# Attention and low-rank mixer on one core: all batches in a replanned order, loads of two queues charged in issue order, early copies on GpSimd

## The chip, the cores and the metric

The kernel runs on 1 core of one Trainium2 chip. The metric is the device time of one execution in microseconds. Several executions are timed and the median is given. A profile of one execution is at hand as well; its times count from the start of the profiled span.

The engines have short names: PE is TensorE (matrix products), ACT is ScalarE, DVE is VectorE, POOL is GpSimd, SP is SyncE. POOL and SP also issue DMA transfers, each on a queue of its own: the casting loads go through POOL's queue, plain copies and stores through SP's.

## What is computed

For 4 batches, 8 heads, 768 positions and head width 64: attention with a local window of 96 keys and 8 global keys, with a bias linear in the distance; then, on the 512-wide rows of all heads, a mixer along the sequence of rank 32 and a two-layer MLP of width 2048, both with a residual.

```python
scores = scale * np.matmul(q, k.transpose(0, 1, 3, 2))
scores = np.where(keep, scores + bias, -1e9)
a = softmax(scores)
x = (a @ v) rearranged to [batch, seq, heads * width]
h = x^T @ U @ V
u = x + h^T
out = u + relu(u @ w_ch1) @ w_ch2
```

Inputs and output are fp32.

## The kernel before

**Tasks.** The kernel is a list of 1107 named tasks. A task is a handful of instructions on one engine, with what it depends on and the buffers that it takes and gives back. `ORDER` is a list of all names, written out. `Planner.run` walks it once, gives every task a start from durations held in the code, chooses buffer slots and PSUM banks on the way, and returns the tasks sorted by those starts; in that order the instructions are issued, so each engine works its own tasks in the order in which `ORDER` has them. Real waits are semaphores that follow from the data. Where the plan shows a gap on PE in the opening, `idle` fills it with matmuls on zeros (line 1327).

**Names.** The work goes over 16 head pairs p (4 a batch), then an MLP a batch b.

- Loads: `lk`, `lq`, `lv` with p, `w1_i`, `w2_i` (quarters of the weights), `mixl` (U and V of the mixer, on SP, behind `back`, which follows `EK1`). Pair 0's k and q come over SP as fp32 and are cast by `Ck0`, `Cq0`; all other loads are casting DMAs issued by POOL. From pair 4 on `lk` and `lq` are two transfers each. Staging buffers hold 3 pairs of k and q and 4 of v.
- Attention: `TK`, `TQ` transpose on PE, `EK`, `EQ` evacuate them, `KO` builds keys with the global ones in front, `VC`, `VG` the same for v. `SB` puts the bias into PSUM (batch 0), `S` adds the scores, `EX` is the exponential on ACT, `MK` the mask (later batches), `PV` the product with v, `RC` reciprocal and `NM` normalization on DVE, `XC` the cast of the result to fp16 (for pair 3 `NH` in three parts).
- Mixer: `UP` starts u in PSUM and forms x U; `TE` evacuates the small product, `HM` multiplies it by V (`vs0`, `vs1`, `vs2` are fp16 halves of V and their difference), `E0`, `E1` evacuate u. `HR` says for each pair whether `HM` uses all 128 rows (F) or 64 (R, two products side by side in the array). 
- MLP: the first layer as plain products `M1` with `RL`, `RM` (ReLU), and from batch 1 partly as seven-product blocks `ZP` with sums on DVE and ACT (`Z...`, `PA`, `PB`, `TW`, `TD`). The second layer is `RS`, then `P1` to `P7` for each of three column tiles t, added to x by `DA` to `DH` on DVE, and stored by `O` on SP. In the last batch, tile 2, `P4` and `DG` are cut in two (`a`, `b`) with stores of their own.

**Which engine.** Strings in `CFG` give, for each pair, the engine of a copy: A is ACT, D is DVE, P is POOL, S a DMA on SP, Q a DMA on POOL. `VO` sets `VC` and `VG`, `XC` the cast of x, `VS` the three vs tasks.

**The plan's DMA model.** A task with a `size` is a transfer. Each of the two queues has a time from which it is free; a transfer on SP also pushes POOL's queue back. The tasks are charged in the order of `ORDER`, not of their starts.

**Array forms.** `S` and `RS` and `HM` in form R use 64 rows, `TK`, `TQ` of pairs 1 to 3 use 64 columns, all else the whole array.

Of the kernel before, what the change touches and what calls it, by code (L numbers as in the profile page):

```python
# [36 lines left out]
XU5 DA0.1 P30.1 DF0.1 mask4 MK6.1 MK6.2 P50.0 lv6 lq9 VC7 TE5 HM5 mask6 KO8 S6.0 EX6.0 E05 P60.0 DB0.0 lk9 mask7
lk10 lv8 P60.1 DB0.1 lv11 S7.1 RS0.2 EX7.1 MK6.0 MK7.0 EX7.2 MK7.2 P10.2 P70.0 TK9 EK9 TQ9 EQ9 MK7.1 VC6 DA0.2 VG6
TQ10 EQ10 P50.1 TK10 EK10 P70.1 DC0.0 lq11 VG7 PV7 DD0.1 KO9 PV6 RC7 NM7 P20.2 XC7 lk11 RC6 NM6 P60.2 DB0.2 P30.2
UP7 XC6 VC8 VG8 P40.1 UP6 P70.2 XE6 XU6 TE6 ZS4 XE7 XU7 lk12 TE7 DD0.0 P40.0 DC0.1 O0.1 HM6 E06 HM7 E17 DF0.2 DG0.1  # L40
ZP11.5 DD0.2 P40.2 ZU1.5 DG0.0 E07 ZT1 S8.0 EX8.0 S8.1 O0.0 EX8.2 EX8.1 KO10 P50.2 M1a1.3 TK11 DC0.2 EK11 O0.3
# [5 lines left out]
RM1.5 ZP51.6 HM8 E08 ZA1.7 ZX1.6 TK12 TD1 EK12 ZP41.7 ZR1.7 M1a1.5 RL1.5 VG9 ZB1.6 ZP51.7 ZB1.7 M1a1.0 ZV1.6 M1b1.0
RL1.0 ZV1.7 ZP31.6 M1a1.1 M1b1.1 MK9.0 lq12 TQ12 ZP31.7 VC11 ZP41.6 VG11 ZD1.6 ZQ1.6 EQ12 ZD1.7 ZQ1.7 RL1.1 ZR1.6
PA1.3 RS1.1 S10.1 EX10.2 EX10.1 PA1.0 PB1.0 S10.0 EX10.0 PB1.3 KO12 P21.1 P11.1 PV9 P51.1 RC9 NM9 PB1.1 DA1.1 S11.0
EX11.0 RS1.0 P21.0 P51.0 P11.0 DA1.0 XC9 S11.1 EX11.2 EX11.1 MK11.0 P31.0 DF1.0 MK11.2 P61.1 MK10.0 UP9 XE9 lq14  # L50
TQ14 EQ14 MK11.1 P31.1 DF1.1 P61.0 DB1.0 XU9 TE9 PV11 RC11 lk14 TK14 EK14 lk15 HM9 DB1.1 P71.0 E09 P71.1 lv14 VC14
# [1327 lines left out]
```

## Time and profile before

| | us |
|---|---|
| median of 3 runs (225.2 to 225.95) | 225.79 |
| the profiled execution | 225.68 |
| its span | 223.9 |
| first filler matmul starts | 0.94 |
| first product (`SB0`) starts | 3.09 |
| last task of batch 0's attention before the MLP (`S4.1`) ends | 30.9 |
| last matmul starts | 220.33 |
| last store lands | 223.0 |

The granted clock of PE is 1.00 over the whole span. The page gives the busy time of each engine, the chain of work that ended last and groups of instructions by line; the timeline gives single instructions in order. Matmuls overlap: one that is shown with 0.326 us starts 0.163 us behind the one before it, so the distance between starts tells more than the busy time. In the waits view a line reads: engine and line, what it waited for, total us, how many times, the longest. In the view by stretches a line has the stretch, its length, then busy time (and instructions) of PE, weight loads, DVE, ACT and POOL, the PE clock, the DMA share and GB/s.

### The profile page before, as it was taken

To read this page: it belongs to the slowest core of one execution; us is meant where nothing else is said; L and a number is where in the kernel's file an instruction comes from. 1 tells how busy PE (TensorE), PEld (TensorE's weight loads), DVE (VectorE), ACT (ScalarE), POOL (GpSimd) and SP (SyncE) were. 2 spreads that over 40 slices of the span, in tenths; PEclk is the share of its full clock that TensorE was granted. 3 is DMA by queue.
4 is the path that set the end of the run, shared out by engine and by line. 5 is a ranking of instruction groups with operands and counts; after the bars stand their busy time and mean duration, and the time that the engine had idled before them with its cause. 6 is when DMAs were issued, how large, how long until landed. Compare 5 with 4: busy or idle time off the path is not lost.

```text
span 223.9 us, 6008 instructions
## 1 busy us (share of the span) xinstructions
PE 217.5 (97%) x2446; PEld 160.8 (72%) x2446; DVE 182.3 (81%) x407; ACT 143.5 (64%) x251; POOL 68.9 (31%) x90
## 2 busy tenths in 40 slices
PE   8997999999999999999999999999999999999993
PEld 3754876675888976666788886666688976658883
DVE  5876957889998887997987888788888995888892
ACT  6889697887877378787855567668732347882000
POOL 8876976634964400191221400012000000000000
PEclk9999999999999999999999999999999999999999
DMA  6999999999999987399090941609100104000035
GB/s 172 174 176 146 181 182 185 193 206 161 169 149 73 157 151 223 97 115 71 0 107 12 108 123 52 200 12 70 39 3 3 47 3 187 0 4 0 0 116 215
DMA packets 88763, 23.97 MB, mean 107 GB/s; under 512 B 76416, under 2 KB 86528, under 8 KB 88736
## 3 DMA queue, kind: packets, MB, share of 16 engines
q0 software_dynamic: 69888, 13.64, 73.8%
q1 hardware_dynamic: 18848, 9.95, 15.7%
q8 instruction: 19, 0.31, 0.6%
q14 instruction: 8, 0.07, 0.1%
HBM read 27.46 MB, written 6.29 MB: 151 GB/s over the span
## 4 chain that ended last, share of the span: by engine, by line
PE 90%; DMA 4%; POOL 2%; issue 1%; ACT 1%; DVE 0%; DVEq 0%; POOLq 0%
PE ps L1226 34%; PE ps L1095 14%; PE ps L1000 13%; PE ps L1024 8%; PE ps L716 4%; DMA stgq<-in_q_dram 4%; PE ps L594 4%; PE ps L822 3%; PE ps L849 2%; PE ps L848 2%; PE ps L946 2%; PE ps L1327 1%; PE ps L1218 1%; PE ps L697 1%; POOL stgk L454 1%
## 5 line engine op out<-in xcount | busy, mean ns | idle before, releaser
L781 ACT ACTIVATE ep<-ps 128x1024 f16<-128x1024 f32 (+1 forms) x48 | 43.9, 952 | 14.8 <-PE ps L716 14.5
L1226 PEld LDWEIGHTS <-htr 128*128 128x128 f16 x392 | 36.2, 98 | 6.7 <-issue 2.3
L1238 DVE TENSOR_TENSOR x_sb<-x_sb,ps 128x256 f32<-128x256 f32 (+1 forms) x60 | 26.9, 464 | 7.5 <-PE ps L1226 7.1
L1000 PE MATMUL ps<-uT,w 128*128 128x384 f16 x176 | 32.4, 326 | 0.0
L1226 PEld LDWEIGHTS <-sA 128*128 128x128 f16 x288 | 27.3, 98 | 3.5
L458 POOL DMA_DIRECT2D vt<-in_v_dram x16 | 16.6, 1046 | 30.7 <-PE ps L849 27.3
L1000 PEld LDWEIGHTS <-w 128*128 128x128 f16 x176 | 16.7, 98 | 10.5
L1226 PE MATMUL ps<-w,sA 128*128 128x256 f16 x192 | 24.2, 273 | 0.0
L1226 PE MATMUL ps<-tB,htr 128*128 128x256 f16 (+1 forms) x200 | 23.8, 268 | 0.0
L1226 PE MATMUL ps<-w,htr 128*128 128x256 f16 x192 | 23.5, 273 | 0.0
L1006 ACT ACTIVATE htr<-ps 128x384 f16<-128x384 f32 x44 | 20.8, 492 | 4.1 <-PE ps L1000 3.5
L454 POOL DMA_DIRECT2D stgk<-in_k_dram x24 | 19.8, 845 | 9.9 <-PE ps L594 5.0
L454 POOL DMA_DIRECT2D stgq<-in_q_dram x24 | 20.0, 844 | 5.6 <-DMA w<-in_moe_w_ch_dram 3.4
L1024 PE MATMUL ps<-uT,w 128*128 128x384 f16 x112 | 21.3, 326 | 0.0
L1113 DVE TENSOR_TENSOR htr<-ps,zu 128x384 f16<-128x384 f32 x30 | 16.1, 554 | 6.1 <-PE ps L1095 4.6
L794 DVE TENSOR_TENSOR ep<-ep,mask 128x1024 f16<-128x1024 f16 x24 | 15.9, 684 | 2.9 <-ACT ep L781 2.9
L359 ACT ACTIVATE zu<-ps 128x384 f32<-128x384 f32 x30 | 14.4, 492 | 4.2 <-PE ps L1095 4.0
L887 DVE TENSOR_TENSOR x_sb<-ps,rcp 128x768 f32<-128x768 f32 x16 | 15.2, 953 | 0.4
L1024 PEld LDWEIGHTS <-w 128*128 128x128 f16 x112 | 10.6, 98 | 6.8
L1095 PEld LDWEIGHTS <-w 128*128 128x128 f16 x108 | 10.1, 98 | 6.2 <-issue 0.3
L1042 ACT ACTIVATE htr<-ps 128x768 f16<-128x768 f32 x14 | 11.3, 811 | 4.7 <-PE ps L1024 4.5
L716 PE MATMUL ps<-qT,kT 64*128 64x128 f16 x192 | 14.0, 217 | 0.0
(127 smaller groups left out, 442.3 us busy)
## 6 DMA issues: line engine op xcount, KB each, us to landing
out_dram<-x_sb SPq DMA_DIRECT2D x17, 256.0 KB, 2.4
w<-in_moe_w_ch_dram POOLq DMA_DIRECT2D x8, 512.0 KB, 10.6
vt<-in_v_dram POOLq DMA_DIRECT2D x16, 192.0 KB, 6.6
stgk<-in_k_dram POOLq DMA_DIRECT2D x24, 96.0 KB, 5.8
stgq<-in_q_dram POOLq DMA_DIRECT2D x24, 96.0 KB, 6.1
out_dram<-x_sb SPq DMA_DIRECT2D x13, 128.0 KB, 1.9
...
```

The source lines that it names most:

```text
L454: nc.gpsimd.dma_start(o[:, i], src[b, h0 + i].rearrange("(n p) d -> p n d", p=P))
L458: nc.gpsimd.dma_start(vt[gv.slot][:, :, :, 0:D], v[b, h0:h0 + 2].rearrange("h (n p) d -> p h n d", p=P),)
L716: nc.tensor.matmul(t[:, hi, j * P:(j + 1) * P], lhs, qt[r, i * P:(i + 1) * P], start=not biased, stop=True, skip_group_check=biased,)
L781: nc.scalar.activation(ep[gep.slot][:, :, lo:512], ps[:, gsc.slot:gsc.slot + 2, lo:512], AF.Exp, scale=qk_scale)
L794: nc.vector.tensor_tensor(ev, ev, mv, ALU.mult)
L1000: nc.tensor.matmul(ps[:, g.slot, 0:HS], w1[:, dc, jt * P:(jt + 1) * P], ub[:, dc, i * HS:(i + 1) * HS], start=(dc == 0), stop=(dc == NDC - 1),
L1006: nc.scalar.activation(htr[:, jt, i * HS:(i + 1) * HS], ps[:, g.slot, 0:HS], AF.Relu)
L1024: nc.tensor.matmul(ps[:, g.slot + half, 0:HS], w1[:, dc, jt * P:(jt + 1) * P], ub[:, dc, half * HS:(half + 1) * HS], start=(dc == flat[0]) ...
L1095: nc.tensor.matmul(bank(g), a()[:, i], bq[:, i], start=first and i == 0, stop=last and i == 1, skip_group_check=True,)
L1113: return lambda: nc.vector.tensor_tensor(o, x(), y(), ALU.add)
L1226: nc.tensor.matmul(o if part is None else o[:, part], a[:, j, c0 + cols.start:c0 + cols.stop], bq[:, j] if part is None else bq[:, j, part ...
L1238: nc.vector.tensor_tensor(o, o, x, ALU.add)
```

## The change

`ORDER` is a new permutation of the same 1107 names, for all batches. In the plan, a transfer may not start before the last one issued on the other queue has started (`issued`), so that a transfer must stand in `ORDER` where it is issued; POOL's queue is taken to be free from 5.6 instead of 6.1. `mixl` stands ahead of `lk4` now, and was behind `w1_2`.

`CFG` moves copies: `VC`, `VG` of pairs 1 and 2, `vs0`, `vs1` and `XC` of pair 2 go to POOL, which made none before; `VC6`, `VG6` go to ACT. Other copies change between ACT, DVE and SP. `HR` turns pairs 0, 2 and 9 from F to R. `RC` of a pair waits for `NM` two pairs earlier (the two share a buffer); both are DVE's. `VS` can name a DMA on POOL, which this setting does not use.

Array forms change 72 times in the new order of PE's tasks and 77 times in the old one.

```diff
--- before.py
+++ after.py
 ORDER = """
-lk0 ones2 wz iota lq0 lk1 ones0 vz relf lq1 rel3 lk3 lq2 bias1 ones3 lv0 bias0 SB0.2 SB0.1 Ck0.1 Cq0.0 bias2 bias4
-Ck0.0 TK0 EK0.1 lk2 Cq0.1 TQ0 EQ0.0 SB0.0 lq3 EK0.0 KO0.1 KO0.0 EQ0.1 mask1 S0.0 EX0.0 TK1 S0.1 EX0.1 EK1 S0.2 KO1
-TQ1 EQ1 ones1 lv1 back SB1.1 TK3 EK3 KO3 VC0 mask5 VG0 EX0.2 lk5 lv3 lv2 lq5 lk4 SB1.2 S1.1 EX1.1 S1.2 TQ2 EQ2 lq4
-SB1.0 w1_0 S1.0 EX1.0 TK2 EK2 KO2 lk7 VC1 w1_3 PV0 RC0 EX1.2 lv4 VG1 TQ3 EQ3 SB2.1 S2.1 EX2.1 lq6 SB2.2 S2.2 EX2.2
-PV1 NM0 SB3.0 S3.0 EX3.0 RC1 NM1 SB2.0 S2.0 w1_2 EX2.0 mixl u16 XC0 VC2 VC3 VG3 SB3.1 S3.1 EX3.1 SB3.2 S3.2 EX3.2
-VG2 vs0 vs1 TK5 EK5 XC1 TQ5 PV2 RC2 NM2 UP0 TE0 TK4 EK4 UP1 TE1 XC2 EQ5 HM0 E00 PV3.0 PV3.1 PV3.2 RC3.2 RC3.0 NH3.2
-TQ4 EQ4 NH3.0 UP2 TE2 HM1 E01 HM2 E02 RC3.1 NH3.1 KO4 NM3 UP3.0 UP3.1 UP3.2 TE3 M1a0.3 M1c0.3 mask0 HM3 E03 KO5 S4.1
-E13 EX4.1 lq7 M1d0.3 TK7 M1b0.3 RL0.3 M1b0.14 M1b0.15 M1a0.2 M1c0.2 M1a0.15 EX4.2 M1a0.13 vs2 TD0 M1a0.14 MK4.2 VC4
-VG4 w1_1 RM0.15 RM0.14 RL0.15 mask2 S4.0 EX4.0 MK4.1 EK7 M1d0.2 M1b0.2 RL0.2 MK4.0 RL0.14 M1b0.13 mask3 KO7 ZS5
-M1a0.10 M1b0.12 RM0.12 RM0.13 RL0.10 TQ6 PV4 M1a0.11 M1b0.11 RL0.13 EQ6 RC4 NM4 XC4 TQ7 EQ7 ZS7 RL0.11 RM0.11 lk6
-lv5 S5.0 S5.1 EX5.0 MK5.0 EX5.2 M1a0.8 M1b0.10 RM0.10 PA0.3 PB0.3 M1a0.9 RL0.9 w2_2 EX5.1 MK5.1 M1b0.5 RM0.5 M1a0.0
...
-M1a3.4 RL3.4 M1b3.5 RM3.5 ZP33.6 RS3.0 ZV3.6 ZD3.6 ZQ3.6 PA3.3 RS3.1 PA3.0 RS3.2 P23.2 P23.0 ZQ3.3 ZQ3.2 P13.1 P13.2
-PA3.1 P13.0 DA3.1 DA3.0 P53.2 P63.0 P53.1 PB3.0 P63.1 P53.0 DA3.2 P63.2 P23.1 PB3.2 PB3.3 DB3.0 PB3.1 DF3.2 P73.0
-DB3.1 P73.1 DB3.2 P33.2 DD3.0 O3.2a O2.0 DC3.0 DC3.2 P33.1 DC3.1 DH3.2 O3.2 DD3.1 P33.0 DF3.1 O3.1 DF3.0 O3.0 P73.2
-DD3.2 O3.5a P43.0 DG3.0 O3.3 P43.1 DG3.1 O3.4 P43.2a P43.2b DG3.2a O3.5b DG3.2b O3.5c
+ones1 wz lk0 iota relf rel3 ones3 lk1 bias1 bias0 SB0.0 lq1 lk3 ones0 lv0 bias2 Ck0.0 bias4 Ck0.1 vz TK0 EK0.0 lk2
+lq2 KO0.0 lv1 lq0 Cq0.1 Cq0.0 SB0.1 SB0.2 TQ0 EQ0.0 lq3 ones2 lv2 EK0.1 KO0.1 EQ0.1 lv3 TK1 EK1 KO1 back S0.1 TQ1
+EQ1 S0.0 mask1 mixl EX0.1 S0.2 TK3 EK3 VC0 KO3 VG0 lk4 EX0.2 lk5 EX0.0 VC1 VG1 lq4 VC2 VG2 vs1 SB1.0 SB1.1 S1.1
+SB1.2 S1.2 EX1.1 S1.0 EX1.0 TK2 EK2 KO2 TQ2 lq5 vs0 w1_3 EQ2 PV0 RC0 SB2.2 EX1.2 NM0 SB2.1 S2.1 EX2.1 XC0 S2.2 EX2.2
+TQ3 EQ3 PV1 RC1 SB2.0 S2.0 EX2.0 NM1 u16 SB3.1 S3.1 EX3.1 XC1 SB3.2 S3.2 EX3.2 SB3.0 S3.0 EX3.0 VC3 VG3 PV2 RC2 UP0
+TE0 mask0 NM2 XC2 TK4 EK4 w1_0 PV3.0 PV3.1 PV3.2 RC3.0 NH3.0 RC3.1 NH3.1 HM0 E00 lv4 RC3.2 NH3.2 UP1 TE1 UP2 TE2 TQ4
+EQ4 TK5 NM3 EK5 HM2 E02 HM1 UP3.0 KO4 UP3.1 UP3.2 TE3 TQ5 E01 EQ5 S4.0 HM3 E03 E13 KO5 EX4.0 w1_2 S4.1 EX4.2 lq7
+M1a0.13 RL0.13 M1a0.14 lk7 M1b0.15 M1a0.15 RL0.14 lq6 vs2 M1b0.14 M1b0.13 M1a0.3 M1c0.3 M1d0.3 w1_1 VC4 VG4 MK4.2
+lv5 mask2 EX4.1 MK4.1 RM0.14 RM0.13 M1b0.12 RL0.15 M1a0.2 M1c0.2 M1b0.3 M1d0.2 M1b0.2 RM0.15 MK4.0 RM0.12 ZS7 PV4
+RC4 TQ7 EQ7 NM4 M1b0.11 mask3 RL0.3 RL0.2 lk6 M1a0.11 TK7 EK7 KO7 M1a0.10 RM0.11 RL0.11 XC4 TQ6 EQ6 ZS5 S5.0 RL0.10
+EX5.0 S5.1 EX5.2 MK5.2 EX5.1 M1b0.8 RM0.8 M1a0.0 w2_2 w2_0 M1c0.0 M1d0.0 M1b0.10 M1a0.6 RM0.10 M1b0.0 M1a0.5 RL0.6
...
+ZV3.3 M1a3.5 ZP73.6 ZP53.6 PB3.2 ZP33.7 ZD3.7 ZX3.6 ZQ3.7 RL3.5 M1a3.1 M1b3.1 ZB3.6 RL3.1 ZP43.6 ZP33.3 ZR3.6 ZV3.6
+M1a3.4 ZP23.6 ZP33.6 ZD3.3 RS3.0 RL3.4 ZV3.7 ZD3.6 ZA3.6 ZQ3.6 PA3.3 RS3.1 O2.0 ZQ3.3 RS3.2 P23.2 ZQ3.2 PA3.1 P23.1
+P23.0 PA3.0 P13.0 DA3.0 P13.2 PB3.1 P13.1 DA3.1 P53.2 P53.0 DA3.2 P63.2 PB3.0 PB3.3 DC3.2 P63.1 DC3.0 P53.1 DC3.1
+DB3.2 P33.1 P33.0 DF3.0 P63.0 DB3.0 O3.0 P33.2 P73.0 DF3.1 DB3.1 O3.1 DD3.0 P73.2 DD3.2 O3.5a DH3.2 P43.0 DG3.0 O3.3
+P73.1 O3.2 DD3.1 P43.2a DF3.2 O3.2a P43.2b P43.1 DG3.2a O3.5b DG3.2b O3.5c DG3.1 O3.4
 """.split()
 CFG = {
...
-    "ZR": "DDAADDDA", "ZQ": "DDAADDDD", "TE": "ADAAAAAAAAAAAADA", "XE": "DDDDDAADADAADAAA", "EK": "ADDDDDADADADDAAD", "EQ": "DDAAAADDAAADDAAD", "KO": "ADDDDDADSSSSASDS",
-    "HR": "FRFRRRRRFFRRFRRR", "IB": "AAAA", "U16": "A", "VS": "DAD", "C0": "ADDADADA", "DL": (), "SPL": (0,), "BI": (0, 1, 2, 3), "EKS": "ADDADADA", "EQS": "DDDADADA", "KOS": "ADDADADA",
-    "VO": "DDDDDDDSSSSSDSSS", "XC": "DDDDDAAADADQADQA", "E": "AAAAAAAAAAAAAAAA",
+    "ZR": "DDDADADA", "ZQ": "DDAADDDD", "TE": "AAADAAADAAAAAAAA", "XE": "DDDDDAAAAAAAAADA", "EK": "ADDDADADAAADDDAD", "EQ": "DDADADDDAAADAAAA", "KO": "ADDDDDSDSASSSSAD",
+    "HR": "RRRRRRRRFRRRFRRR", "IB": "AAAA", "U16": "D", "VS": "PPD", "C0": "ADAADADA", "DL": (), "SPL": (0,), "BI": (0, 1, 2, 3), "EKS": "DADADADA", "EQS": "DADADADA", "KOS": "DADADADA",
+    "VO": "DPPDDDASSSSSSSDS", "XC": "DDPDDDDADQDQDAAD", "E": "AAAAAAAAAADAAAAA",
 }
 
 
@@ -166,8 +166,9 @@
         clock = {PE: 0.0, ACT: 2.0, DVE: 0.7, POOL: 0.75, SP: 0.7}
         lanes = {POOL: [0.0] * self.LANES, SP: [0.0] * self.LANES}
         mode = 0
-        dma_free = {POOL: 6.1, SP: 0.0}
+        dma_free = {POOL: 5.6, SP: 0.0}
         shared_port = {POOL: [], DVE: []}
+        issued = {POOL: 0.0, SP: 0.0}
         for t in (self.names[n] for n in names):
             r = 0.0
             for d in t.deps:
@@ -180,7 +181,7 @@
                     for i in range(g.slot, g.slot + g.n):
                         self.free[g.kind][i] = 1e9
             if t.size:
-                r = max(r, lanes[t.eng][t.parts - 1])
+                r = max(r, lanes[t.eng][t.parts - 1], issued[POOL if t.eng == SP else SP])
             s = max(r, clock[t.eng])
             if t.eng == PE and t.mode != mode:
                 s = max(s, clock[PE] + self.switch)
@@ -225,6 +226,7 @@
                     shared_port[POOL].append((begun, t.end, 1 if t.size else 2))
             clock[t.eng] = t.end
             if t.size:
+                issued[t.eng] = max(issued[t.eng], s)
 
                 begin = max(t.end + 1.6, dma_free[t.eng])
                 other = POOL if t.eng == SP else SP
@@ -514,8 +516,10 @@
     def build_vs(g):
         def go():
             o, v1, v2 = vs[VR[g]:VR[g] + R, g], vf[:, 0:HS], vf[:, HS:S]
-            e = ENG[CFG["VS"][g]]
-            if g < 2:
+            e = ENG.get(CFG["VS"][g])
+            if e is None:
+                nc.gpsimd.dma_start(o, moe_V[:, g * HS:(g + 1) * HS])
+            elif g < 2:
                 copy(e, o, v2 if g else v1)
             else:
                 (nc.gpsimd if e == POOL else nc.vector).tensor_tensor(o, v1, v2, ALU.subtract)
@@ -530,11 +534,12 @@
     c_vz = add(DVE, 0.55, lambda: nc.vector.memset(vs, 0.0), name="vz")
     c_vs = []
     for g in range(3):
-        ve = ENG[CFG["VS"][g]]
+        vq = CFG["VS"][g] == "Q"
+        ve = POOL if vq else ENG[CFG["VS"][g]]
         c_vs.append(
             add(
-                ve, ({DVE: 0.93, POOL: 1.2} if g == 2 else {DVE: 0.35, ACT: 0.46, POOL: 0.55})[ve], build_vs(g),
-                [c_mixl, c_vz], fast=1, name=f"vs{g}",
+                ve, 0.6 if vq else ({DVE: 0.93, POOL: 1.2} if g == 2 else {DVE: 0.35, ACT: 0.46, POOL: 0.55})[ve], build_vs(g),
+                [c_vz] if vq else [c_mixl, c_vz], size=0.2 if vq else 0.0, fast=1, name=f"vs{g}",
             )
         )
 
@@ -556,6 +561,7 @@
     c_tb = [add(tw, td_, build_t(g, 1), [c_ta[g]], fast=12, name=f"TWb{g}") for g in range(2)]
 
     mm1_done, osb_done, ut_done, tmp_done = {}, {}, {}, {}
+    nm_done = {}
     m2_done, kept, zt_read, plain_mm = {}, {}, [], {}
 
     def attention(p):
@@ -870,7 +876,7 @@
                         rcp[p % 2][:, :, 2 * s:2 * s + 2].unsqueeze(3).broadcast_to((P, 2, 2, D)), ALU.mult,
                     )
 
-                RCs.append(add(DVE, 0.2, rcs, [PVs[s]], br=[gpv], name=f"RC{p}.{s}"))
+                RCs.append(add(DVE, 0.2, rcs, [PVs[s], nm_done.get(p - 2)], br=[gpv], name=f"RC{p}.{s}"))
                 NHs.append(add(DVE, 0.44, nms, [RCs[s]], acq=[gx16], rel=[gpv], name=f"NH{p}.{s}"))
                 UPs.append(
                     add(
@@ -890,6 +896,7 @@
 
         if split:
             NM = add(DVE, 0.96, norm, RCs + xw, rel=[gpv], name=f"NM{p}")
+            nm_done[p] = NM
             UP = UPs[-1]
         else:
             def pv_all(steps=tuple(PVs)):
@@ -899,8 +906,9 @@
             PV = add(
                 PE, 0.68, pv_all, MKs + VO, lat=0.3, acq=[gpv], rel=geps + [gv], name=f"PV{p}"
             )
-            RC = add(DVE, 0.23, rc, [PV], name=f"RC{p}")
+            RC = add(DVE, 0.23, rc, [PV, nm_done.get(p - 2)], name=f"RC{p}")
             NM = add(DVE, 0.96, norm, [RC] + xw, rel=[gpv], name=f"NM{p}")
+            nm_done[p] = NM
             xq = CFG["XC"][p] == "Q"
             xe = POOL if xq else ENG[CFG["XC"][p]]
```

More of the change, by code (lines that the diff above doesn't have):

```diff
@@ L37 @@
[L37 to L41, printed above, removed]
@@ L47 @@
[L47 to L51, printed above, removed]
@@ new lines @@
+DB0.1 P60.0 mask7 mask6 MK7.0 S7.1 EX7.1 MK7.1 RS0.2 EX7.2 MK7.2 P30.2 P50.1 VC6 VG6 P20.2 TK9 EK9 P10.2 TQ9 PV7
+DC0.0 MK6.1 DB0.0 O0.0 TQ10 P70.1 EQ9 DA0.2 KO9 EQ10 RC7 lk11 NM7 TK10 EK10 P60.2 MK6.0 PV6 DF0.2 P70.0 DD0.1 KO10
+P40.1 XC7 UP7 RC6 NM6 XC6 UP6 DB0.2 P70.2 XE7 XU7 lq11 XE6 XU6 TE6 DD0.0 lv10 P40.0 DG0.1 DC0.1 TE7 HM6 VC11 VC8 E06
+TD1 HM7 E17 DD0.2 DG0.0 ZP11.5 ZU1.5 P40.2 E07 ZT1 S8.0 S8.1 EX8.0 P50.2 DC0.2 O0.1 M1a1.3 EX8.2 TK11 EX8.1 DG0.2
+EK11 ZP11.4 ZU1.4 M1b1.3 ZP21.5 O0.2 TQ11 ZA1.5 O0.4 RL1.3 ZP61.4 ZW1.4 EQ11 ZP21.4 ZA1.4 ZP61.5 ZW1.5 MK8.0 VG8
@@ new lines @@
+M1b1.1 KO12 ZX1.6 ZB1.6 ZV1.7 ZP31.6 ZP31.7 ZV1.6 RL1.0 VC9 MK9.0 ZD1.6 RL1.1 ZD1.7 ZP41.6 ZR1.6 ZQ1.6 ZQ1.7 PA1.0
+lq14 S10.0 EX10.0 S10.1 EX10.2 RS1.1 P21.1 VG9 PV9 PA1.3 RC9 NM9 VG11 XC9 P11.1 DA1.1 EX10.1 MK10.1 PB1.0 PB1.3 lv14
+S11.0 EX11.0 RS1.0 P51.0 MK11.0 P11.0 DA1.0 S11.1 EX11.2 EX11.1 MK11.1 P61.1 DB1.1 P21.0 MK11.2 lq15 TQ14 EQ14 P31.0
+P31.1 DF1.0 UP9 DC1.0 P71.1 PV11 XE9 XU9 TK14 EK14 DF1.1 TE9 RC11 KO14 NM11 P61.0 DB1.0 P51.1 HM9 E09 S12.0 lk13
+EX12.0 RS1.2 MK10.0 DC1.1 P71.0 MK10.2 DD1.0 DD1.1 P11.2 DA1.2 S12.1 EX12.1 P41.0 DG1.0 EX12.2 P21.2 VC10 VG10 PV10
@@ new lines @@
+TK13 RC10 XC11 UP11 NM10 XE11 XC10 P61.2 XU11 TE11 P31.2 UP10 XE10 EK13 TQ13 EQ13 DB1.2 MK12.0 MK12.2 P71.2 DF1.2
+DD1.2 XU10 TE10 P41.1 DG1.1 S14.0 HM11 HM10 TD2 E010 E011 E111 EX14.0 O1.0 P51.2 lk15 ZT2 P41.2 DG1.2 DC1.2 S14.1
+EX14.1 EX14.2 M1a2.5 M1b2.5 ZP12.6 ZU2.6 lv12 VC12 RM2.5 M1a2.1 TK15 RL2.5 EK15 ZP62.6 ZW2.6 ZP22.6 M1a2.4 ZP12.7
+MK12.1 MK14.2 ZP72.6 MK14.0 ZU2.7 ZP52.6 ZX2.6 RL2.4 ZB2.6 ZV2.6 M1b2.4 RM2.4 ZA2.6 M1b2.1 ZP42.6 TQ15 VG12 ZR2.6
+ZP32.6 ZD2.6 EQ15 ZP62.7 M1a2.3 O1.3 KO15 ZW2.7 RL2.1 lv13 MK14.1 ZP22.7 O1.4 ZA2.7 M1b2.3 PV12 RC12 RL2.3 ZP72.7
@@ new lines @@
+M1a2.0 M1b2.0 ZX2.7 ZP42.7 RL2.0 O1.2 ZP12.4 VC14 O1.1 VG14 ZR2.7 O1.5 NM12 KO13 ZP52.7 PV14 ZU2.4 XC12 UP12 ZB2.7
+ZP32.7 RC14 XE12 ZV2.7 NM14 ZP62.4 ZD2.7 ZQ2.7 ZP12.5 ZW2.4 ZP52.4 ZU2.5 XU12 TE12 ZP22.4 ZA2.4 ZP72.4 ZP22.5 ZA2.5
+ZP62.5 ZX2.4 ZB2.4 ZW2.5 M1a2.7 RL2.7 ZP42.4 PA2.0 HM12 ZP72.5 E012 M1a2.2 M1b2.2 ZP52.5 XC14 ZX2.5 ZP32.4 ZR2.4
+UP14 ZQ2.6 PA2.3 RL2.2 ZB2.5 ZV2.5 ZP42.5 ZR2.5 M1a2.6 RL2.6 XE14 ZP32.5 XU14 TE14 M1b2.7 RM2.7 M1b2.6 RM2.6 ZD2.4
+ZD2.5 ZQ2.5 ZV2.4 ZQ2.4 PA2.2 PA2.1 RS2.1 HM14 E014 RS2.0 P12.0 DA2.0 PB2.0 P12.1 DA2.1 P22.1 PB2.1 S13.1 EX13.2
@@ new lines @@
+PB2.3 P22.0 VC13 VG13 EX13.1 P52.1 PB2.2 P62.1 P62.0 S15.1 EX15.2 EX15.1 MK13.2 lv15 VC15 DB2.1 P32.1 P32.0 DB2.0
+P72.0 MK13.1 DF2.1 DF2.0 MK15.1 P72.1 DD2.1 S15.0 EX15.0 S13.0 EX13.0 RS2.2 P32.2 P12.2 MK15.2 VG15 MK15.0 PV15
+MK13.0 PV13 DA2.2 P62.2 P52.2 P22.2 DC2.1 O2.1 RC13 NM13 XC13 UP13 XE13 RC15 DB2.2 P72.2 NM15 XC15 UP15 DD2.0 P42.0
+ZS3.2 DD2.2 XE15 XU15 TE15 ZS3.3 XU13 TE13 P42.1 DF2.2 HM15 E015 HM13 E013 P42.2 P52.0 ZP13.5 E115 DG2.2 ZT3 DG2.1
+TD3 ZP13.4 M1a3.0 ZU3.5 DG2.0 M1b3.0 ZP23.2 ZP63.5 ZU3.4 ZP63.4 ZP23.4 ZA3.4 RL3.0 ZW3.4 ZP13.2 ZP13.3 ZP73.4 ZP53.4
```

46 lines of the change are left out of this document (15 added, 31 removed).

## The prediction

> **What bounds the kernel now.** I read the page's first section, then its chain, then the matrix engine's waits, then the busy time by stretches, and last the timeline of the first 31 us and of the end.
>
> ```profile
> PE 217.5 (97%) x2446; PEld 160.8 (72%) x2446; DVE 182.3 (81%) x407; ACT 143.5 (64%) x251; POOL 68.9 (31%) x90
> PE 90%; DMA 4%; POOL 2%; issue 1%; ACT 1%; DVE 0%; DVEq 0%; POOLq 0%
> ```
>
> The matrix engine is the bound. A busy PE is not a streaming one here, so I also took the distance between consecutive matmul starts from the trace. From 30.9 us to the last matmul (220.33) no distance is over its streaming time by more than 0.18 us, and the large ones are all at changes between full-array and 64-row products: 0.098 going in, 0.121 coming out. There is no wait left there to remove. All waits lie in the opening:
>
> ```profile
> PE ps L594 <- DMA stgq<-in_q_dram: 1.5, 1, 1.5
> PE ps L1327 <- POOL zero L376: 0.9, 1, 0.9
> PE ps L575 <- DMA stgq<-in_q_dram: 0.5, 1, 0.5
> ...
> 0.00:11.20 11.20, 10.13 (x114) 6.03 (x115) 7.69 (x25) 8.54 (x15) 9.35 (x21) 1.00 1.11 173
> 11.20:22.40 11.20, 9.52 (x166) 5.46 (x165) 7.74 (x19) 10.13 (x12) 8.01 (x10) 1.00 2.32 161
> 22.40:33.60 11.20, 10.86 (x171) 8.91 (x172) 8.60 (x23) 8.51 (x15) 9.59 (x13) 1.00 1.69 181
> 33.60:44.80 11.20, 11.20 (x117) 7.27 (x116) 9.18 (x23) 9.43 (x19) 7.25 (x9) 1.00 1.64 189
> ```
>
> By start distances the opening loses: 1.71 us at 20.97 (TQ5 waits for lq5), 0.65 at 14.01 (TQ3 for lq3), some 0.4 in two smaller gaps, and 4.55 in 42 filler matmuls (L1327), of which 2.15 before the first product. The two load waits are the large items:
>
> ```profile
> 20.69 0.51 PE L594 MATMUL ps<-ident,stgk 128*128 128x128 f16 x6
> 22.74 0.50 PE L594 MATMUL ps<-ident,stgq 128*128 128x128 f16 x6 [1.55 <-DMA stgq<-in_q_dram]
> ...
> 12.86 1.76 POOL L454 DMA_DIRECT2D stgq<-in_q_dram  x2
> ```
>
> lq5 was issued at 12.86 and landed at 22.60. The load queue is full and goes in order: in the landing records each load ends one service time after the one before it, 1.0 us for a k or q of pairs 1 to 3, 1.3 for later ones (two parts), 1.27 for a v, 2.55 for a quarter of w1. Only from 12.31 (lk2) to 21.31 (lv2) did five loads that should take 6.1 us take 9.0: mixl's two transfers, issued by SP at 11.12 and landed by 19.10, cost that queue 2.9 us. The old ORDER lists mixl far behind those loads, so its plan did not charge them.
>
> **The change part by part.**
>
> *Opening.* The first eight queued loads are the same set in another order, ending with lq3. They ended at 16.09 before, so lq3 lands about 16.1, at most 17.5 if the earlier mixl (behind KO1, about 9.7 instead of 11.12) puts all its 2.9 us ahead of it. Behind them come lv2, lv3, lk4 (21.3, the same bytes as before up to lv2), lk5, lq4 and lq5 (24.6, the old end of that set). I followed the new order of each engine with the durations of the old rows. SB0.0 now goes first and needs the whole of rel3 (done 3.30): start 3.4 against 3.09. TQ0 needs both casts of q, now both on ACT: 5.03 + 2 x 0.53 = 6.1, start 6.3, as before. EX0.1 starts at 8.35 (old first exp 8.04), because S0.1 waits on ACT's EK0.1, KO0.1, EQ0.1 (0.49 + 0.62 + 0.50). PE is through S2.2 at 15.45 and waits for lq3 until 16.25, so the 0.65 wait stays as 0.8; PV1 ends at 17.55, as before. Then the gain begins: S3.0 ends at 20.35 (the old scores at 20.69), PV2 and UP0 follow, TK4 at 21.8 finds its load, PV3 starts behind the last exp at 22.35 (old 25.74), and TQ5 comes only behind UP3.2, at about 27 with lq5 in since 24.6. So the 1.71 goes. What is late next is UP2, behind the cast XC2, now on GpSimd.
>
> *GpSimd's copies* are not in the old trace: VC1, VG1, VC2, VG2 (660 elements), vs0, vs1 (384), XC2 (768). The nearest row of that engine is:
>
> ```profile
> 0.92 0.33 POOL L378 IOTA early<- 128x256 int32 x1
> ```
>
> With some 0.1 fixed (its smallest memsets take 0.10), that is 0.9 ns an element: 0.69, 0.45 and 0.79 us, 4.45 for all seven. Lower bound: DVE's rows for the same copies, 0.33, 0.33 and 0.55, sum 2.5. Upper bound: each is held off once by DVE. That happens in the trace:
>
> ```profile
> 3.89 0.36 DVE L361 CAST stgk<-sA 128x384 f16<-128x384 f32 x1 [0.59 <-DMA sA<-in_k_dram]
> 5.03 0.69 DVE L361 CAST stgq<-sA 128x384 f16<-128x384 f32 x1 [0.78 <-DMA sA<-in_q_dram]
> ```
>
> The same cast takes 0.33 longer while GpSimd issues lv0 (4.47 to 5.53). Another 0.4 on each of seven is 2.8, so 7.3 in all. I take 4.45, as most of DVE's work in that stretch reads PSUM, and the slow pairs are fast SBUF copies. GpSimd then does VC1, VG1 behind lv1 (about 15 to 16), lq4 (1.66), VC2, VG2, vs1, lq5 (1.66), vs0, w1_3 (0.8), and ends XC2 between 23.35 and 24.75. Queued behind those copies are lq4, lq5, w1_3 and w1_0. Their issue moves to 17, 20.5, 22 and 24.5; that costs the queue at most 0.7 us of emptiness, w1_3 lands near 27.8, w1_0 near 30.3, and PE asks for them at 29.2 and 33. I take UP2 at 24.8, 0.85 behind UP1.
>
> From there DVE sets the pace (NM3 0.93, EK5 0.55, KO4 0.73, TE3 0.29, EQ5 0.54, E03 0.56), and the first M1 product starts at 29.2, with XC2 early 28.4, with lq3 late 29.8. The old kernel ended S4.1 at 30.93, with 0.65 of M1 done and 0.2 of S4.0 open: the same point is 30.5. **Gain 1.3 us, bounds 0.7 and 2.1.** The three saved switches and the shorter HM0 and HM2 are inside it.
>
> *Half-array HM.* HR turns pairs 0, 2 and 9 from F to R. F is two 384-column matmuls at 0.163 (0.33); R takes 0.17 for both (30.22 to 30.39). Outside the opening only HM9 counts: 0.16.
>
> *Switches.* Counting tasks in the two orders, 77 changes of array form become 72: 30 to 27 up to S4.1, 47 to 45 later. Two at 0.11: 0.22.
>
> *End.* The last product was half of P4 with a 128-column addition and a 64 KB store; now it is P43.1 with DG3.1 and the 256 KB O3.4. Old: last matmul start to end of span, 223.9 - 220.33 = 3.57. New, from the old DG3.1 and O3.4: 0.32 to the addition, 0.42 for it, 2.06 until landed (220.12 to 222.18), and the 0.9 from last landing to end: 3.70. Loss 0.15.
>
> *Moved copies between ACT and DVE, and the waits of RC on NM two pairs earlier:* nothing. The first lie under a PE that has no wait after 30.9 us; if that cover goes, see the last rival. RC and NM both run in order on DVE. The planner's edits issue nothing; they set start times, so slots, order and fillers.
>
> **Sum:** -1.3 - 0.16 - 0.22 + 0.15 = -1.5. The profiled execution took 225.68 (span 223.9 and 1.8 around it), 0.1 under the median of 225.79. So 224.2.
>
> **Rivals.**
> *The load wait only moves.* Queue bytes are unchanged, and lq3 is now the last of its eight. For it: the wait before TQ3 stays in my own working. Against it: TQ5, the worse one, goes 4 us behind its load. If lq3 is at 17.5 and the exps drift with it, the gain shrinks to 0.3 or less: 225.5.
> *GpSimd held off (slower).* XC2 stands behind six copies and four issues, and PE has UP2 ahead of TQ4, TK5, HM2 and UP3, so its delay goes to the M1 stage one for one. It decides from 1.5 us over my 4.45, a third more. At the upper bound, 2.8 less the 1.3 gained gives +1.5, less 0.23 for the rest: 226.9. For it: the 0.69 row. Against: few fast DVE copies are left there, as VC1, VC2 and the vs copies themselves leave DVE.
> The Trainium skill (SBUF — State Buffer, "Who interferes with whom") has this as a rule: the port pair that VectorE and GpSimd share is locked for a whole instruction and the other blocks fully, in a two-port mode. The 0.36 and 0.69 rows agree with it. By the Trainium skill (GPSIMD Engine Reference, "Engine selection") one-input work runs at about line rate, which at that page's 1.2 GHz would be an estimate of 0.55 us for 660 elements and bring the sum to about 223.5, with UP2 right behind UP1.
> *All fits better.* lq3 at 16.1 or before, XC2 early: gain 2.1 and the rest: 223.4 or less.
> *A new wait after 31 us.* Replanned batches lose cover once, about 2 us (the size of the one wait above): 226.2. Against: the old order has none in 190 us.
>
> **How the numbers follow.** Forecast 0.50 (its own range 223.4 to 225.0), better 0.12, wait only moves 0.18, GpSimd held off 0.14, new wait 0.06. A measurement of this kernel can tell about 0.3%, 0.68 us. Faster by more: 0.62; within: 0.18; slower: 0.20. The range 222.8 to 226.4 holds the first three, most of the last and little of the slow GpSimd case.
>
> **What would show it.** Right: no wait over 0.3 us before TQ5; PV3 near 22.4; first M1 product near 29.2; copies on GpSimd near 0.7; tail 3.7 behind the last matmul. Wrong: copies over 0.95, UP2 later than 26.3, a wait for q over 1.5 us at TQ3, or any PE gap over 0.3 us after 31 us.

## The result, and the profile after

The changed kernel took 227.0 us (median; 226.22 to 229.12) against 225.41 for the kernel before on the same chips: a ratio of 1.0076 with a 95% interval of 1.0052 to 1.0099. It is slower by about 1.7 us, where 224.2 was forecast. The profiled execution took 227.80 us with a span of 226.0; before it was 225.68 and 223.9. Three executions that ran far longer than the others of their kernel (230.0 us in w1_3_first, 250.96 in only_vc1_pool, 770.06 in one_copy_old_end_r) are in no ratio below, and as they are the profiled ones of these three kernels, the experiments read no trace of them.

First the page's section of busy times and its chain of waits, for the changed kernel:

```profile
PE 215.6 (95%) x2409; PEld 158.1 (70%) x2409; DVE 183.5 (81%) x397; ACT 142.7 (63%) x254; POOL 74.1 (33%) x97
PE 66%; DMA 25%; POOL 5%; issue 2%; ACT 0%; DVE 0%; POOLq 0%; SPq 0%
```

PE was 90% of the chain and is 66% now; transfers went from 4% to 25%. The matrix engine is no longer what ends last in a part of the span. The waits of PE, and the stretches that the prediction showed:

```profile
PE ps L854 <- DMA vo<-vt: 1.1, 1, 1.1
PE ps L722 <- DVE kO L363: 0.9, 1, 0.9
...
PE ps L722 <- DMA kO<-kT: 0.5, 1, 0.5
PE ps L600 <- DMA stgq<-in_q_dram: 0.5, 1, 0.5
PE ps L1008 <- DMA w<-in_moe_w_ch_dram: 0.4, 1, 0.4
PE ps L828 <- POOL x L367: 0.4, 1, 0.4
```

```profile
0.00:11.20 11.20, 8.74 (x87) 4.18 (x87) 7.47 (x23) 8.56 (x16) 9.59 (x21) 1.00 1.10 169
11.20:22.40 11.20, 9.97 (x193) 6.47 (x193) 10.80 (x18) 9.05 (x11) 9.53 (x13) 1.00 1.96 150
22.40:33.60 11.20, 10.10 (x140) 7.28 (x138) 7.11 (x19) 9.23 (x16) 9.21 (x13) 1.00 1.27 138
33.60:44.80 11.20, 10.75 (x113) 7.22 (x112) 8.90 (x24) 8.37 (x15) 8.45 (x10) 1.00 1.90 177
56.00:67.20 11.20, 10.72 (x132) 8.88 (x127) 10.91 (x23) 7.73 (x13) 7.75 (x10) 1.00 2.30 153
67.20:78.40 11.20, 10.13 (x149) 8.94 (x147) 7.12 (x14) 8.75 (x13) 7.74 (x10) 1.00 1.78 144
```

The 1.5 us wait for a q in the opening is gone. In its place stand waits for transfers, and three of them lie behind 31 us, where there were none: by the distance between matmul starts 0.62 us at 37.9 (TQ7 for lq7), 0.64 at 58.0 (S6 for KO6) and 1.24 at 72.5 (PV7 for VG7). In the rows from 22.4 to 33.6 us the transfers moved 138 GB/s against 181 before.

How these hang together is to be read from the chain of waits in order of time (start, duration, what), 9 to 74 us:

```profile
9.01 9.90 DMA vt<-in_v_dram
...
18.96 0.73 POOL vo L367
...
20.55 0.72 POOL vs L367
21.27 1.73 POOL stgq L456 x2
...
26.78 10.37 DMA w<-in_moe_w_ch_dram
...
40.80 10.42 DMA w<-in_moe_w_ch_dram
...
51.50 11.75 DMA vt<-in_v_dram
63.31 6.55 DMA vo<-vt
69.88 3.82 DMA vo<-vt
```

Read downwards: lv2 lands at 18.9; GpSimd has waited for it and copies VC2, VG2 and vs1; only then does it issue lq5, and after two more copies w1_3 and w1_0; the load queue, which is served in order, carries that lateness through w1_2, w2_0 and lv7; VC7, the SP transfer of pair 7's v, can start only then; VG7 is issued when VC7 has landed; and PV7 stands until 73.7 us. From 9 to 73.7 us the path runs through loads, through GpSimd, which issues them, and at the end through two SP transfers.

Where the span's 2.1 us come from: the first M1 product starts at 30.14 us instead of the old equivalent 30.5 (-0.36); the three waits behind it, +2.5; last matmul start to end of span 3.89 instead of 3.57, +0.3; the rest, -0.3, is about what the half-array HM9 and the fewer switches were to save, but was not measured by itself. All of this is one execution of each kernel. How far single executions differ is seen in ko6_on_dve and vo7_on_dve below, which have the same tasks in the same order up to M1: there the first M1 product started at 28.83 and 28.91 us.

### The profile page after: what moved, and what is told of

Same layout as the page of the kernel before. It is cut to its first block, busy times and chain, and to the rows that moved or that the text cites. A ratio compares the mean times of both kernels' runs of the same rounds, so it can differ in the third digit from the quotient of the medians.

```text
span 226.0 us, 5936 instructions
## 1 busy us (share of the span) xinstructions
PE 215.6 (95%) x2409; PEld 158.1 (70%) x2409; DVE 183.5 (81%) x397; ACT 142.7 (63%) x254; POOL 74.1 (33%) x97
## 4 chain that ended last, share of the span: by engine, by line
PE 66%; DMA 25%; POOL 5%; issue 2%; ACT 0%; DVE 0%; POOLq 0%; SPq 0%
PE ps L1234 28%; PE ps L1103 14%; DMA vt<-in_v_dram 10%; DMA w<-in_moe_w_ch_dram 9%; PE ps L1008 6%; PE ps L1032 6%; DMA vo<-vt 5%; PE ps L722 3%; PE ps L600 2%; PE ps L828 2%; PE ps L855 2%; PE ps L854 1%; DMA sA<-in_k_dram 1%; POOL vt L460 1%; PE ps L954 1%
## 5 line engine op out<-in xcount | busy, mean ns | idle before, releaser
L1008 PEld LDWEIGHTS <-w 128*128 128x128 f16 x176 | 16.6, 98 | 11.0 <-DMA w<-in_moe_w_ch_dram 0.6
L1032 PEld LDWEIGHTS <-w 128*128 128x128 f16 x112 | 11.0, 98 | 7.1
L1103 PEld LDWEIGHTS <-w 128*128 128x128 f16 x108 | 10.3, 98 | 6.6 <-issue 0.3
L722 PE MATMUL ps<-qT,kO 64*128 64x128 f16 x160 | 12.5, 218 | 1.7 <-DVE kO L363 0.9
```

Source lines behind the costliest of these rows:

```text
L722: nc.tensor.matmul(t[:, hi, j * P:(j + 1) * P], lhs, qt[r, i * P:(i + 1) * P], start=not biased, stop=True, skip_group_check=biased,)
L1008: nc.tensor.matmul(ps[:, g.slot, 0:HS], w1[:, dc, jt * P:(jt + 1) * P], ub[:, dc, i * HS:(i + 1) * HS], start=(dc == 0), stop=(dc == NDC - 1),
L1032: nc.tensor.matmul(ps[:, g.slot + half, 0:HS], w1[:, dc, jt * P:(jt + 1) * P], ub[:, dc, half * HS:(half + 1) * HS], start=(dc == flat[0]) ...
L1103: nc.tensor.matmul(bank(g), a()[:, i], bq[:, i], start=first and i == 0, stop=last and i == 1, skip_group_check=True,)
```

## The experiments

Four theories. **Queue:** what GpSimd's copies cost is GpSimd's time, since its loads stand behind them. **Lock:** VectorE and GpSimd hold each other off in their copies. **SP:** the SP transfers behind the full load queue (KO6, VC7) are themselves the cause. **Order:** the new order costs, with or without the copies. Each run's ratio is to the kernel before, timed beside it.

**The copies taken back.**

```diff
-    "VS": "PPD", "VO": "DPPDDDASSSSSSSDS", "XC": "DDPDDDDADQDQDAAD"
+    "VS": "DAD", "VO": "DDDDDDASSSSSSSDS", "XC": "DDDDDDDADQDQDAAD"
 ORDER: VC1 VG1 behind RC0, VC2 VG2 ahead of VC3, vs0 behind VG3, vs1 ahead of TE0
```

> The changed kernel with its seven GpSimd copies given back to DVE and ACT (VC1, VG1, VC2, VG2, vs0, XC2 to DVE, vs1 to ACT), all else and all other orders kept. Queue theory (the copies stand between the loads on GpSimd, the load queue runs empty for 3.6 us up to w1_0, and late loads are what PE waits for at 29.5, 37.9, 58.0 and 72.5): w1_0 lands at 30.5 or earlier instead of 33.3, w2_3 at 54.5 or earlier instead of 57.2, no PE wait over 0.3 us after 31 us, KO2 near 0.9 instead of 1.83, time about 224.7. SP theory (the new copies on SP's queue, KO6 and VC7, are what is waited for): the waits at 58.0 and 72.5 stay, about 226. Order theory (the new order of the loads empties the queue by itself): w1_0 still lands after 32, 226.3 or more.

225.58 us, ratio 0.9997 (0.9963 to 1.003); the profiled execution 224.54. The loss is gone, and with it the theory that the order alone costs. So is the SP theory: KO6 and VC7 still go over SP here, and PE waits for neither. But the median is 0.9 us above the 224.7 expected: level with the kernel before, not under it. The page's chain for this kernel:

```profile
PE 93%; DMA 3%; ACT 1%; DVE 1%; POOL 1%; issue 0%; POOLq 0%
```

w1_0 lands at 30.17 instead of 33.31, lv7 at 59.94 instead of 63.25. VectorE's two copies of KO2, in the timelines of the changed kernel and of this one:

```profile
14.12 1.83 DVE L363 COPY kO<-kT 128x480 f16<-128x480 f16 x2
```

```profile
13.98 0.44 DVE L362 COPY kO<-kT 128x480 f16<-128x480 f16 x2
```

The 1.83 us lie under GpSimd's VC1 and VG1 (14.27 to 15.88). So the lock exists too, and the next runs had to part the two. In the changed kernel PE had made up for it soon: its products start 1.16 us later than those of no_pool_copies at 16.0 us, and 0.61 us earlier at 21.2.

**One load ahead of the copies.**

```diff
 ORDER: w1_3 moved from behind vs0 to behind lk5
```

> The changed kernel with the issue of w1_3 moved ahead of the first copy on GpSimd (behind lk5); copies stay on GpSimd. Queue theory: the queue holds 2.55 us more work while the copies run, w1_0 lands at 31 or earlier, the waits at 37.9 and 72.5 shrink, KO2 stays at 1.8: 225.5 to 226.2. SP theory: unchanged, about 227. Order theory: gains as much as taking the copies away.

226.37 us, 1.0023 (0.9995 to 1.0051): 0.2 us above the band, between the changed kernel and the one without copies. One load early brings back more than half of the loss by the two ratios, though all copies stay.

**One half of the copies, and the other.**

```diff
 vc1_on_dve:     "VO": "DDPDDDASSSSSSSDS"; ORDER: VC1 VG1 behind RC0
 only_vc1_pool:  "VO": "DPDDDDASSSSSSSDS", "VS": "DAD", "XC": "DDDDDDDADQDQDAAD"; ORDER: VC2 VG2 vs0 vs1 as in no_pool_copies
```

> The changed kernel with one of the five GpSimd copies taken back: VO of pair 1 (two 128x660 copies) on VectorE, behind RC0. GpSimd keeps VO of pair 2, both VS copies and XC2. Lock theory (VectorE is held off by the two copies at 14.27 us, and the 1.12 us wait of S2 for kO at 14.7 us is the main loss): KO2 falls from 1.83 to about 0.44 us, S2's wait goes, and the median falls by about 1.0 us to 225.9-226.1. Queue theory (the loss is the loads that GpSimd issues behind its copies): GpSimd still waits for lv2 before VO of pair 2 and issues the same loads behind it, so w1_3 still lands near 29.5-30.1 and the waits at 38, 58 and 72 us stay; S2's wait goes, but PE only comes earlier to the same late loads: 226.4-226.9.

> The other half: VO of pair 1 alone stays on GpSimd, and VO of pair 2, both VS copies and XC2 go back to VectorE and ScalarE. Queue theory: GpSimd no longer waits for lv2 in the middle of its loads; w1_3 lands before 28.6, w1_0 near 30.5, w2_3 before 54.5, the waits of PE at 38, 58 and 72 us are under 0.3 us, and the median is 225.5-226.2. Lock theory: KO2 still takes about 1.8 us and S2 still waits about 1.1 us, and the median stays at 226.5-227.0.

vc1_on_dve: 226.2 us, 1.0035 (1.0005 to 1.0065), between the two expectations. The wait for KO2 went; w1_3 landed at 27.71 rather than 29.5 to 30.1, so my queue figure was wrong there. GpSimd reached VC2 1.5 us earlier, but not because VC1 was gone: lv2, for which it waits in both kernels, landed at 17.36 instead of 18.91. VC7 was still issued at 61.28, and PV7 still waited 1.1 us. only_vc1_pool: 225.08 us, 0.9981 (0.9949 to 1.0013): 0.4 us below the queue theory's band, on the side away from the lock theory's 226.5. So VC1 and VG1 may stay at no cost that can be told, and those that hold up lq5, w1_3 and w1_0 are the dear ones. That VC1 and VG1 lock VectorE in this setting too is read from one_copy_old_end below, which has the same copies.

**KO6 off the SP queue.**

```diff
-    "KO": "ADDDDDSDSASSSSAD"
+    "KO": "ADDDDDDDSASSSSAD"
```

> The changed kernel with KO of pair 6 copied on VectorE instead of by an SP transfer; the GpSimd copies stay. SP theory (the transfer behind the full load queue is itself what costs): the wait of S6 at 58 us goes and nothing takes its place, 226.0-226.4. Queue theory: that wait (0.6 us) goes, but the loads stay late and the VO transfer of pair 7 at 72 us takes over what was gained: 226.5-227.0.

228.09 us, 1.0103 (1.0051 to 1.0156): slower than either theory had it. In the waits of PE, and in the timeline of VectorE:

```profile
PE ps L854 <- DVE ep L795: 2.1, 2, 1.8
```

```profile
48.28 0.42 DVE L362 COPY kO<-kT 128x480 f16<-128x480 f16 x2 [3.35 <-ACT kT L360]
```

VectorE works in order. Put there, KO6 stands ahead of the last mask of pair 5: VectorE waits 3.35 us for KO6's input, the mask waits behind it, and PV5 stands 1.98 us. What it waits for is ACT's evacuation of the transposed k:

```profile
47.42 0.83 ACT L360 ACTIVATE kT<-ps 128x768 f16<-128x768 f16 x1
```

That is not the late load: the k of pair 6 had landed at 45.59, PE transposed it at 46.42 without a wait, and in no_pool_copies, where the loads are early (42.91), ACT comes to the same task at 46.74. So the place in VectorE's order costs here, and the run says little of the SP theory: the wait of S6 did go, as both theories had it. In the changed kernel KO6's two transfers on SP landed at 57.52 and 58.62, just behind w2_3 (57.16), and cost PE 0.64. On ACT, KO6 finds no room in PSUM in the plan, so there is no such kernel.

**The copies put into the old order.**

```diff
 before.py
-    "VS": "DAD", "VO": "DDDDDDDSSSSSDSSS", "XC": "DDDDDAAADADQADQA"
+    "VS": "PPD", "VO": "DPPDDDDSSSSSDSSS", "XC": "DDPDDAAADADQADQA"
 ORDER: mixl behind back, VC1 VG1 behind lk4, VC2 VG2 vs1 vs0 behind w1_0, lq6 w1_2 behind XC2
```

> The kernel before, its own order, with the same five copies given to GpSimd: VO of pairs 1 and 2, two VS copies, XC2; lq6 and w1_2 stand behind XC2, the rest of the loads keep their places. If the copies cost by themselves (queue and lock theories together): loads from w1_0 on land 2 to 4 us later than in the kernel before, PE waits 0.5 us or more for a load after 27 us, and the median is 1 to 2 us above the kernel before, 226.4-227.5. Order theory (the new order is what costs, with or without the copies): within 0.5 us of the kernel before, 225.0-226.0.

227.55 us, 1.0101 (1.0068 to 1.0134): the copies, with the loads and mixl moved as the edit shows, cost 2 us without the new order. But not by the wait that I expected. No product waits for a load behind 27 us; the waits of PE show the reverse side of one in-order engine for loads and copies:

```profile
PE ps L847 <- POOL vo L364: 1.7, 1, 1.7
```

Here the copy is late behind the loads (VC1 starts at 16.81, behind lk4), and PV1 waits for it. Nor does pair 7 pay here: the old order has lv7 right behind w2_3 (landed at 55.87), the new one has lv6, lk8 and lq8 in between. So where the copies are paid for depends on the order, and the late wait at pair 7 was seen with the new one alone.

**GpSimd busy with nothing.** This separates the queue from the lock: no copy on GpSimd, but time taken from it in front of w1_3.

```diff
 no_pool_copies
+    def busy():
+        for _ in range(21):
+            nc.gpsimd.iota(spare, pattern=[[1, 48]], base=0, channel_multiplier=-1)
+    add(POOL, 3.0, busy, [c_wz], name="busy")
 ORDER: busy ahead of w1_3
```

> The kernel without GpSimd copies (no_pool_copies), with GpSimd made to count into a small tile that nobody reads, 21 short instructions of about 0.14 us, 3.0 us in all, between the issue of lq5 and that of w1_3. No copy changes its engine, nothing waits for the tile. Queue theory (what the copies cost is GpSimd's time ahead of its loads): w1_3 is issued near 24 instead of 20.9 and lands near 30 instead of 27.6, M1 waits 0.4-0.8 us for it, later loads stay 2 to 3 us late, PE waits again at 38, 58 or 72 us, and the median is 1.0 to 1.6 us above no_pool_copies, 226.6-227.2. Lock theory (the loss is that VectorE and GpSimd hold each other off in their copies): nothing copies on GpSimd here, so 225.3-225.9.

229.38 us, 1.0178 (1.014 to 1.0217). Two things went otherwise: each instruction took 0.26 us, 5.5 us in all, and the plan, told of 3.0 us, put 67 filler matmuls on PE:

```profile
21.39 4.11 PE L1340 MATMUL ps<-zero 128*128 128x128 f16 x67
```

PE worked through them while the products behind were ready (the last exponential ended at 22.6), so this run tells nothing of the queue alone. Once more with 11 instructions and 0.1 us in the plan:

```diff
-        for _ in range(21):
+        for _ in range(11):
-    add(POOL, 3.0, busy, [c_wz], name="busy")
+    add(POOL, 0.1, busy, [c_wz], name="busy")
```

> gpsimd_busy_3us once more, with 11 of the counting instructions (2.9 us at the 0.26 us that each took there) and the plan told 0.1 us, so that it places no filler matmuls for them. The fillers, the copies and every engine's order are those of no_pool_copies; GpSimd is 2.9 us late with w1_3 and all that it issues behind. Queue theory: w1_3 issued near 23.8 and landed near 30, w1_0 near 32.8, no filler run of 4 us at 21 us; PE waits for w1_3 and later for what comes behind it (pair 7, about 70 us); median 1.0 to 1.6 us above no_pool_copies, 226.6-227.2. Lock theory: 225.3-225.9.

227.23 us, 1.0086 (1.0058 to 1.0114), at the top of the queue theory's band: the changed kernel's loss, with no copy on GpSimd and VectorE's KO2 at 0.62. In GpSimd's timeline and in the waits of PE:

```profile
20.79 3.40 POOL L381 IOTA spare<- 128x48 int32 x11
```

```profile
PE ps L859 <- DMA vo<-vt: 0.9, 1, 0.9
```

w1_0 landed at 32.88, lv7 at 63.08, and PV7 waited 1.1 us by its start distances, all within 0.5 us of the changed kernel. PE did not wait for w1_3 here (it landed at 29.67, M1 began at 30.92): the late loads are paid at pair 7, nearly 50 us behind the place of their delay. Product by product against no_pool_copies, this profile is 1.5 us later from 9.4 us on, ahead of the busy instructions, which start at 20.79 (0.6 of it from the first transpose); the wait at pair 7 is the only later step over 0.25 us. So the trace shows 1.1 us from the busy instructions. By the two ratios they cost some 2.0; where the rest lies, these traces do not show.

**VO of pair 7 off the SP queue.**

```diff
-    "VO": "DPPDDDASSSSSSSDS"
+    "VO": "DPPDDDADSSSSSSDS"
 ORDER: VC7 VG7 behind DB0.1
```

> The changed kernel with VO of pair 7 copied on VectorE (behind DB0.1, near 67 us, where it has 0.8 us of idle time) instead of by the SP transfer that stands behind the late lv7; the five GpSimd copies stay. If a wait behind the late loads is paid where it stands (queue theory as the last runs left it): PV7's 1.24 us at 72.5 us goes, nothing takes its place, since the loads behind pair 7 have slack, and the median falls by about 1 us to 225.8-226.2. If another late load takes over, as with KO of pair 6: 226.6-227.2.

225.84 us, 1.0022 (1.0002 to 1.0041), in the first band: 1.2 us of the loss come back with all five copies still on GpSimd, the size of PV7's wait. VectorE does the copy at 65.4 us in time that it had:

```profile
65.42 1.07 DVE L362 COPY vo<-vt 128x660 f16<-128x660 f16 x2
```

What is left against no_pool_copies, 0.25% or 0.6 us, is the size of the wait for KO6, which is still there (0.63 at 56.4 us); the two intervals overlap, so that this is a guess.

**Towards a better kernel.** One copy on GpSimd, and the last products in the old order; then pairs 8 and 12 of HR also as R; then VO of pair 7 on VectorE.

```diff
 one_copy_old_end:    only_vc1_pool; ORDER ends ... P43.0 DG3.0 O3.3 P43.1 DG3.1 O3.4 P43.2a DF3.2 O3.2a P43.2b DG3.2a O3.5b DG3.2b O3.5c
 one_copy_old_end_r:  the same, "HR": "RRRRRRRRRRRRRRRR"
 one_copy_end_vo7:    one_copy_old_end, "VO": "DPDDDDADSSSSSSDS"; ORDER: VC7 VG7 behind DB0.1
```

> Only VO of pair 1 on GpSimd (only_vc1_pool) and the end of the kernel before: P43.1, DG3.1 and the 256 KB store O3.4 ahead of P43.2a and P43.2b, so that the last store is 64 KB again. If the end is worth what the spans say (3.9 us in the changed kernel against 3.6 from last matmul start to end of span): the tail is 3.55-3.65 us and the median 0.1-0.3 us under only_vc1_pool, 224.8-225.0, below the kernel before. If the tail does not follow the order of the last products: 3.7-3.9 us, and 225.0-225.2.

> one_copy_old_end with the last two pairs of HR that are F (8 and 12) turned to R: two 384-column matmuls each become 64-row ones side by side. By the streaming time that the three pairs of the change saved (0.53 us for 0, 2 and 9): 0.3 us less streaming, and one to four more changes of array form at 0.11 us: between 0.35 us faster and 0.15 us slower than one_copy_old_end, 224.5-225.1.

> one_copy_old_end with VO of pair 7 on VectorE as in vo7_on_dve. With one GpSimd copy the loads are early enough that PV7 did not wait in that profile, so if the transfer only costs behind a late lv7: within 0.3 us of one_copy_old_end, 225.0-225.4. If PV7's wait also comes up in part of the executions, where the opening is later: 224.6-225.0 and less spread.

225.32 us, 0.997 (0.9944 to 0.9995); 225.39 us, 0.9989 (0.9968 to 1.0009); 225.31 us, 0.9975 (0.9949 to 1.0001). The first two lie 0.1 and 0.3 us above their bands. The first is clear of the changed kernel; under the kernel before it is by 0.3%, with an interval that just leaves out 1, and as the best of several settings that is weak. The old end brought nothing: 3.87 us from last matmul start to end of span. More R changed nothing that can be told. And where lv7 is early (59.00 in one_copy_old_end), taking VC7 off SP changes nothing, as expected. The waits of PE in one_copy_old_end begin with

```profile
PE ps L721 <- DVE kO L362: 1.1, 1, 1.1
```

This is the lock, at the full size that it has in the changed kernel (KO2 1.93 us), in the kernel with the lowest ratio of the study. Against no_pool_copies PE is 1.15 us behind at 16.0 us and 0.54 at 17.1, and these 0.54 us stay: M1 begins at 30.09 against 29.58, with w1_3 in since 26.2. The medians do not show them.

## Why the prediction was wrong

**The step that failed** is the sentence on what stands behind the copies: "that costs the queue at most 0.7 us of emptiness, w1_3 lands near 27.8, w1_0 near 30.3". They landed at 30.10 and 33.31, and the queue lost 1.9 us ahead of w1_3 (25.68 to 30.10, less 2.55 of transfer) and 0.7 ahead of w1_0. Three things were missing. GpSimd waits for lv2 in front of VC2; I had the copies of pair 2 run as soon as lq4 was issued, and lost the 1.49 us that this timeline row of GpSimd shows:

```profile
18.96 1.52 POOL L367 COPY vo<-vt 128x660 f16<-128x660 f16 x2 [1.49 <-DMA vt<-in_v_dram]
...
23.49 0.76 POOL L505 DMA_DIRECT2D w<-in_moe_w_ch_dram  x1
```

lv2 itself landed 3.94 us behind lq3, where a v takes 1.27 in a stream: mixl's two transfers (10.14 to 18.42) fall into that time, while the prediction had looked for them ahead of lq3.

Second, issues at 23.49 and 25.02 instead of my 22 and 24.5 are too late by more than they look: on an empty queue a quarter of w1 takes 5.4 us from issue to landing (24.25 to 29.67 in gpsimd_busy_unplanned, 26.04 to 31.50 in gpsimd_busy_3us), against 2.55 in a stream, so by this estimate an issue has to be at least 2.9 us ahead of the queue's end, and w1_3's was 2.2. That is not the whole: it would have w1_3 in at 28.9, and w1_0 was issued 5.1 us before w1_3 had landed. With the same opening, w1_3 took 5.5 us in vo7_on_dve (22.74 to 28.22) and 6.4 in ko6_on_dve (22.41 to 28.79). Where the other 1.2 us of w1_3 and the 0.7 of w1_0 went stays open. Third, I followed the queue only to the first two quarters of w1 and asked when PE needs those. The queue never caught up: w2_3 came at 57.16 against 52.53 before and 53.43 in no_pool_copies, and pair 7 paid. The sum has no term for anything behind 31 us but HM9, the switches and the end; there the three waits, 2.5 us, stand in its place.

**The sum, term by term.** *Opening, -1.3:* -0.36. Without the copies it is -0.9 (M1 at 29.58), inside my bounds, but so it is, at -1.6, with all copies in ko6_on_dve and vo7_on_dve, so that a single profile does not tell what the copies cost the opening; the TQ5 wait went as forecast, and lq3 was better than forecast (14.97 instead of 16.1), so the rival of the moving load wait fell. *GpSimd's copies, 0.69, 0.45 and 0.79 us:* about right in size. Two copies of 660 took 1.61 and 1.52, the vs copies 0.72 and 0.49, XC2 0.84; XC2 ended at 25.09 and UP2 followed there, against 24.8. Their own duration was not the matter, their place in front of the loads was. *HM9 and switches, -0.38:* about -0.3, as the remainder of the sum. *End, +0.15:* +0.3. SP issues the last four stores one behind the other, 0.5 us apart, and O3.4 went out 0.24 us behind its addition.

**The rivals.** The one on the slower side had GpSimd held off by VectorE, so that XC2 and UP2 come late. XC2 came about 0.3 us late, and it was VectorE that was held off (1.83 against 0.44 us). The Trainium skill (SBUF — State Buffer, "Who interferes with whom") says that whoever issues first has the shared port pair for the whole instruction; the KO2 rows of ko6_on_dve and vo7_on_dve agree on VectorE's side: the first of the two copies, begun 0.11 and 0.03 us before VC1, took 0.31 us, and the second, begun under VC1, ended 0.06 us behind it. In the changed kernel the first began 0.15 us before VC1 and still took 1.15; GpSimd was issuing lk5 at that moment (13.46 to 14.35), and that the issue held the ports is likely but not shown by this row. The direction that I chose was the wrong one. It hardly mattered for the time: one_copy_old_end has the lock and no loss. The rival that came about is "a new wait after 31 us", with its size (2 us, 226.2) near the 2.5 measured. That is luck: the price was that of another wait, and the ground, replanned batches that lose cover, is not the late queue. I gave it 0.06 and argued against it from the old order's 190 us without waits. That was no evidence: the old order had no copies in front of its loads. The mark "any PE gap over 0.3 us after 31 us", named as what would show the forecast wrong, is what the trace shows three times.

**What stays open.** The profiled execution of no_pool_copies took 224.54 us, near my 224.2 and 1.1 under that of the kernel before, yet its median is level with before: what the new order gains in that profile is not in the median. Its executions spread from 224.24 to 226.87, those of the kernel before beside it from 224.88 to 227.62. One thing that differs between executions, the landing of pair 0's q, is in the last section, but it does not set the start of M1 by itself: with q at 5.67 and at 4.92 us M1 started at 28.83 and 28.91 (ko6_on_dve, vo7_on_dve), and with q at 5.39 at 30.14 in the changed kernel. The cause stays open.
